# Seven products of quarters in place of eight for part of the second expert layer's first matrix

## The chip, the cores and the metric

The kernel runs on one core of a Trainium2 chip. The metric is the device time of one execution in microseconds (us), taken as the median over runs. TensorE multiplies matrices into PSUM; VectorE, ScalarE and GpSimd work on vectors; SyncE issues most DMAs. In the rows PE is TensorE's matmul, PEld its weight load, DVE is VectorE, ACT ScalarE, POOL GpSimd, SP SyncE.

## The reference

Windowed attention gives x with 2304 tokens of 512 features; two expert layers follow. The change lies in the second one:

```python
def _moe_ref(x, w_gate, w_val, w_out, rms_g):   # first layer, d_ff = 1536
    xn = x / sqrt(mean(x * x, -1) + 1e-06) * rms_g
    g = xn @ w_gate
    return (g * sigmoid(g) * (xn @ w_val)) @ w_out

def _moe2_ref(x, w_in, w_out, alpha):           # second layer, d_ff = 2048
    h = x @ w_in
    g = np.maximum(h, 0.0) + alpha * np.minimum(h, 0.0)
    return g @ w_out
```

## The kernel before

Every float32 matrix is held as a high and a low half in float16, and a product is three matmuls: high by high, high by low, low by high. Tokens go in blocks of up to 384 columns. Slot ("A", j, c) computes chunk c of the first layer for block j: 24 matmuls (`mm1`), then a chain over ACT, DVE (L921, L922), ACT (L924, high half) and POOL (L930, low half), then the output matmuls (`mm2`) two slots later. Weight blocks sit in slots of one SBUF buffer, `wb`.

The last stretch, the **end part**, does the second layer for the last 1024 tokens. It takes them as four pairs of 128-token tiles (t = 0 to 3) and the 2048 hidden features as eight pairs of 128-feature pieces (cp = 0 to 7), so 32 units in all. For each unit `mm3_t` multiplies by `w_in`: two pieces by 256 tokens, 12 matmuls of 256 columns for each piece. Where the two token tiles lie apart (t = 2), it is 24 matmuls of 128 columns for each piece. Then `mi` (L1080, ACT) and L1084, L1085 (DVE) apply the activation into a tile `fa`; L1086 to L1089 (DVE) form sums of quarters; L1092, L1094 (ACT) write high halves and L1093 (DVE), L1095 (POOL) low halves. `mm4_t` multiplies by `w_out` with seven products of quarters (Winograd's form of Strassen's scheme), 21 matmuls of 256 columns, three units later (`LAGT`). `out_t` (L1120 to L1127) joins the results of a token pair and writes them. `remake` prepares `w_out` for it once for each cp: two POOL adds (L1039, L1040), four DVE subtractions into `s` (L1042 to L1045), an ACT copy (L1048) and a DVE pass (L1049). These eight preparations run under the last "A" slots, one for each slot. `fa` has two buffers, `s` (tag `yb`) one, the PSUM pool `p3` four banks.

The order on each engine is made by a scheduler from the order of the code and its own estimates. The matmul calls of all stages have one line, L97.

## Time and profile before

| | us |
|---|---|
| median of 3 runs (954.62 to 957.86) | 954.78 |
| the profiled execution | 955.83 |
| its span | 953.9 |
| PE busy / DVE / ACT / POOL | 906.1 / 639.4 / 548.2 / 319.2 |

The span is the time from the first to the last instruction in the trace; 1.9 us of the profiled execution lie around it, and this execution is 1.05 us above the median. Rows below give starts in us from the beginning of the span.

### The profile page before, as it was taken

What the parts mean: (1) busy time and instruction counts of PE and PEld (TensorE: products, weight loads), DVE (VectorE), ACT (ScalarE), POOL (GpSimd) and SP (SyncE); (2) the same over time, 40 slices, a digit from 0 to 9 for tenths busy, and PEclk for the clock granted to TensorE, in tenths of its full rate; (3) what the DMA queues carried; (4) which work ended last, traced back from release to release, by engine and by line L of the source; (5) the groups of instructions that cost most, each with busy time, mean ns of one, the idle gap of its engine ahead of it and who ended that gap; (6) DMA issues with size and microseconds to landing.
All of it is one profiled execution on the core that took longest, in us unless ns stands there. A gap on an engine that the chain in (4) does not pass through costs nothing.

```text
span 953.9 us, 18814 instructions
## 1 busy us (share of the span) xinstructions
PE 906.1 (95%) x6760; PEld 618.7 (65%) x6760; DVE 639.4 (67%) x1569; ACT 548.2 (57%) x1537; POOL 319.2 (33%) x324
## 2 busy tenths in 40 slices
PE   6558799999999999999999999999999999999997
PEld 3447676775556676555555555555775558889986
DVE  5999897999777655554664765334545837777674
ACT  3426587766799967767665777544524324444342
POOL 2212441131354544332333233232253622322221
PEclk9687899999999999999999999999999999999999
DMA  9992446545436554544454653322301001000000
GB/s 255 324 360 81 120 132 188 142 157 140 81 72 108 98 103 77 123 83 95 110 90 74 114 106 72 67 59 42 55 14 23 1 1 35 1 23 24 2 24 23
DMA packets 191613, 88.14 MB, mean 92 GB/s; under 512 B 176800, under 2 KB 180384, under 8 KB 191520
## 3 DMA queue, kind: packets, MB, share of 16 engines
q1 hardware_dynamic: 189504, 83.27, 37.8%
q10 hardware_dynamic: 2016, 3.67, 1.1%
q8 instruction: 53, 0.87, 0.4%
q14 instruction: 40, 0.33, 0.1%
HBM read 55.32 MB, written 6.55 MB: 65 GB/s over the span
## 4 chain that ended last, share of the span: by engine, by line
PE 81%; DVE 9%; DMA 3%; issue 3%; ACT 1%; SPq 1%; POOL 1%; DVEq 0%; POOLq 0%; ACTq 0%
PE psw L97 40%; PE acc L97 24%; PE p L97 17%; DVE wb L232 2%; DVE wb L233 1%; DVE wb L231 1%; DVE wb L409 1%; SPq L629 1%; DMA wb<-in_q_dram 1%; PE psw L639 1%; DMA gs<-in_moe_rms_g_dram 1%; POOL ms L737 1%; ACT s L589 0%; DMA rkv<-in_v_dram 0%; DMA pT<-phl 0%
## 5 line engine op out<-in xcount | busy, mean ns | idle before, releaser
L97 PEld LDWEIGHTS <-wb 128*128 128x128 f16 (+1 forms) x4866 | 453.7, 99 | 196.3 <-DVE wb L233 18.6
L97 PE MATMUL psw<-xyall,wb 128*128 128x384 f16 (+1 forms) x2784 | 428.2, 304 | 2.0 <-DVE sqo L284 1.2
L97 PE MATMUL acc<-wb,hlall 128*128 128x512 f16 x822 | 197.6, 379 | 0.8 <-DVE yhl L965 0.6
L97 PEld LDWEIGHTS <-hlall 128*128 128x128 f16 x822 | 79.4, 98 | 80.7 <-POOL hlall L930 1.1
L930 POOL TENSOR_TENSOR hlall<-t,hlall 128x384 f16<-128x384 f32 (+1 forms) x58 | 58.4, 1007 | 148.5 <-ACT hlall L924 130.7
L97 PE MATMUL acc<-wb 128*128 128x512 f16 (+1 forms) x402 | 82.8, 351 | 16.2 <-DVE wb L233 16.1
L97 PE MATMUL p<-xyall,wb 128*128 128x256 f16 (+1 forms) x960 | 88.7, 251 | 0.0
L1095 POOL TENSOR_TENSOR wb<-fa,wb 128x640 f16<-128x640 f32 x32 | 45.5, 1422 | 111.4 <-ACT wb L1094 108.5
L97 PE MATMUL p<-wb 128*128 128x256 f16 x672 | 77.6, 273 | 0.0
L920 ACT ACTIVATE t<-psw,tsc 128x384 f32<-128x384 f32 (+1 forms) x84 | 44.1, 525 | 56.0 <-PE psw L97 54.9
L921 DVE SCALAR_TENSOR_TENSOR t<-t,psw 128x384 f32<-128x384 f32 (+1 forms) x84 | 41.1, 489 | 48.6 <-ACT t L920 48.6
L589 ACT ACTIVATE s<-s,mx 96x128 f32<-96x128 f32 (+2 forms) x132 | 50.1, 380 | 19.9 <-DVE mx L581 18.2
L404 ACT ACTIVATE wb<-wb,wsg 128x512 f16<-128x512 f32 x68 | 46.3, 710 | 16.8 <-DVE wsg L341 10.2
L1093 DVE SCALAR_TENSOR_TENSOR wb<-fa,wb 128x384 f16<-128x384 f32 x32 | 40.5, 1269 | 22.2 <-ACT wb L1092 22.1
L1094 ACT ACTIVATE wb<-fa 128x640 f16<-128x640 f32 x32 | 23.5, 735 | 55.0 <-DVE fa L1087 55.0
L705 POOL TENSOR_TENSOR phl<-s,phl 96x512 f16<-96x512 f32 (+2 forms) x33 | 35.8, 1084 | 57.6 <-ACT phl L699 40.8
L930 POOL TENSOR_TENSOR hlall<-p,hlall 128x256 f16<-128x256 f32 (+1 forms) x49 | 39.3, 805 | 45.1 <-ACT hlall L987 42.0
L985 DVE SCALAR_TENSOR_TENSOR p<-m,oma,psw 128x256 f32<-128x256 f32 (+1 forms) x64 | 34.7, 542 | 26.7 <-ACT m L984 25.3
L407 POOL TENSOR_TENSOR wb<-wb 128x512 f16<-128x512 f32 x28 | 37.3, 1337 | 42.8 <-ACT wb L406 17.2
L930 POOL TENSOR_TENSOR wb<-t,wb 128x256 f16<-128x256 f32 (+1 forms) x26 | 27.2, 1047 | 71.5 <-ACT wb L924 71.5
L233 DVE SCALAR_TENSOR_TENSOR wb<-wb 128x512 int32<-128x512 int32 (+1 forms) x56 | 49.7, 891 | 0.3
L924 ACT ACTIVATE hlall<-t 128x384 f16<-128x384 f32 (+1 forms) x58 | 27.7, 477 | 37.8 <-DVE t L922 37.8
(201 smaller groups left out, 1320.0 us busy)
## 6 DMA issues: line engine op xcount, KB each, us to landing
wb<-in_moe_w_out_dram SPq DMA_DIRECT2D x28, 512.0 KB, 4.7
wb<-in_moe_w_in_dram SPq DMA_DIRECT2D x16, 512.0 KB, 3.8
wb<-in_moe_w_gate_dram SPq DMA_DIRECT2D x12, 512.0 KB, 6.7
wb<-in_moe_w_val_dram SPq DMA_DIRECT2D x12, 512.0 KB, 6.8
...
```

The source lines that it names most:

```text
L97: nc.tensor.matmul(o, a, b, start=start, stop=stop)
L233: nc.vector.scalar_tensor_tensor(w, r[:, :, :, 0], 29, w, ALU.logical_shift_right, ALU.bitwise_or)
L404: nc.scalar.activation(half(b, 0), dec(b), ACTF.Copy, scale=wsg[:, s:s + 1])
L407: nc.gpsimd.tensor_tensor(half(b, 1), dec(b), half(b, 0), ALU.subtract)
L589: nc.scalar.activation(s[:nq, h, :nk], s[:nq, h, :nk], ACTF.Exp, bias=mx[:nq, 1, h:h + 1], scale=-1.0, accum_out=g["dn"][:nq, h])
L705: nc.gpsimd.tensor_tensor(phl[:nq, 1, :, :nk], g["s"][:nq, :, :nk], phl[:nq, 0, :, :nk], ALU.subtract)
L920: nc.scalar.activation(t[:, :T], pg[:, :T], ACTF.Tanh, scale=tsc[:, chunk(c):chunk(c) + 1])
L921: nc.vector.scalar_tensor_tensor(t[:, :T], t[:, :T], 1.0, pg[:, :T], ALU.add, ALU.mult)
L930: nc.gpsimd.tensor_tensor(a[:, 1, :T], t[:, :T], a[:, 0, :T], ALU.subtract)
L985: nc.vector.scalar_tensor_tensor(p[:, :T], m[:, :T], oma[:, c:c + 1], ps[:, :T], ALU.mult, ALU.add)
L1093: nc.vector.scalar_tensor_tensor(l[:, 0:3], f[:, 0:3], 0.25, h[:, 0:3], ALU.mult, ALU.subtract)
L1095: nc.gpsimd.tensor_tensor(l[:, 3:8], f[:, 3:8], h[:, 3:8], ALU.subtract)
```

## The change

For cp = 2, 3, 4 (`SEVEN`) `mm3_t` no longer does eight products of quarters but seven (`seven`): 42 matmuls of 128 columns into two PSUM banks, `pa` and `pb`. ACT copies one product out (L1119) and DVE adds the others up (L1120 to L1123) into the `fa` tile; the activation then reads that SBUF tile. The scheme needs combinations of the weights, once for each of the three cp (`remake_in`), and of the tokens, once for each t (`remake_y`: the low half of these is made on POOL). For t = 0 these are made together with the eight old preparations, now twelve in all, and three of the last "A" slots may take two; for t = 1 to 3 the tokens are prepared at cp = 5 of the pair before. One of the five buffers for the halves of a unit moves to `hlall`, and f[:, 7] is computed from other, equal terms.

```diff
@@ -1050,6 +1050,79 @@
         ts[cp] = [x.rearrange("p (a c) -> p a c", a=4) for x in (h, l)]
 
 
+    SEVEN = range(2, 5)
+    ws, yt4, slot_of = {}, {}, {}
+
+    def split4(s, eng=nc.vector):
+        at_ = one_slot(), one_slot()
+        h, l = (wb16[:, i * 1024:(i + 1) * 1024] for i in at_)
+        sv = s.rearrange("p a c -> p (a c)")
+        nc.scalar.activation(h, sv, ACTF.Copy)
+        eng.tensor_tensor(l, sv, h, ALU.subtract)
+        r = [x.rearrange("p (a k c) -> p a k c", a=4, c=128) for x in (h, l)]
+        for x, i in zip(r, at_):
+            slot_of[id(x)] = i
+        return r
+
+    def remake_in(cp):
+
+        c, c_ = b_i(2 * cp), b_i(2 * cp + 1)
+        f = tail["tl"].tile([128, 4, 256], F32, tag="fa", bufs=2, name="f")
+        s = tail["tl"].tile([128, 7, 256], F32, tag="yb", bufs=1, name="s")[:, 0:4]
+        fv = f.rearrange("p a c -> p (a c)")
+        nc.gpsimd.tensor_tensor(fv[:, 0:512], half(c, 0), half(c, 1), ALU.add)
+        nc.gpsimd.tensor_tensor(fv[:, 512:1024], half(c_, 0), half(c_, 1), ALU.add)
+        a11, a12, a21, a22 = (f[:, i] for i in range(4))
+        nc.vector.tensor_tensor(s[:, 0], a21, a22, ALU.add)
+        nc.vector.tensor_tensor(s[:, 1], s[:, 0], a11, ALU.subtract)
+        nc.vector.tensor_tensor(s[:, 2], a11, a21, ALU.subtract)
+        nc.vector.tensor_tensor(s[:, 3], a12, s[:, 1], ALU.subtract)
+        ws[cp] = split4(s)
+
+    def y_parts(t):
+        (j0, n0), (j1, n1) = tiles[2 * t:2 * t + 2]
+        return [xy[j % NXY][:, :, :, n * 128:n * 128 + 128] for j, n in ((j0, n0), (j1, n1))]
+
+    def remake_y(t):
+
+        f = tail["tl"].tile([128, 2, KD, 128], F32, tag="fa", bufs=2, name="f")
+        s = tail["tl"].tile([128, 7, 256], F32, tag="yb", bufs=1, name="s")[:, 0:4]
+        for i, y in enumerate(y_parts(t)):
+            nc.gpsimd.tensor_tensor(f[:, i], y[:, 0], y[:, 1], ALU.add)
+        b11, b12, b21, b22 = (f[:, i, 2 * k:2 * k + 2].rearrange("p a c -> p (a c)") for k in range(2) for i in range(2))
+        nc.vector.tensor_tensor(s[:, 0], b12, b11, ALU.subtract)
+        nc.vector.tensor_tensor(s[:, 1], b22, s[:, 0], ALU.subtract)
+        nc.vector.tensor_tensor(s[:, 2], b22, b12, ALU.subtract)
+        nc.vector.tensor_tensor(s[:, 3], b21, s[:, 1], ALU.subtract)
+        yt4[t] = split4(s, nc.gpsimd)
+
+    def seven(t, cp):
+        pa = tail["ps3"].tile([128, 4, 128], F32, tag="p3", name="pa")
+        pb = tail["ps3"].tile([128, 4, 128], F32, tag="p3", name="pb")
+        y0, y1 = y_parts(t)
+        c, c_ = b_i(2 * cp), b_i(2 * cp + 1)
+        w, y = ws[cp], yt4[t]
+        for o, wl, yl in (
+                (pa[:, 0], lambda l, k: blk(c, l)[:, k], lambda l, k: y0[:, l, k]),
+                (pa[:, 1], lambda l, k: blk(c, l)[:, 2 + k], lambda l, k: y0[:, l, 2 + k]),
+                (pa[:, 2], lambda l, k: w[l][:, 1, k], lambda l, k: y[l][:, 1, k]),
+                (pb[:, 1], lambda l, k: w[l][:, 0, k], lambda l, k: y[l][:, 0, k]),
+                (pb[:, 2], lambda l, k: w[l][:, 2, k], lambda l, k: y[l][:, 2, k]),
+                (pb[:, 0], lambda l, k: blk(c_, l)[:, 2 + k], lambda l, k: y[l][:, 3, k]),
+                (pb[:, 3], lambda l, k: w[l][:, 3, k], lambda l, k: y1[:, l, 2 + k])):
+            n = 0
+            for k in range(2):
+                for l, m in ((0, 0), (0, 1), (1, 0)):
+                    mm(o, wl(l, k), yl(m, k), n == 0, n == 5)
+                    n += 1
+        f = tail["tl"].tile([128, 8, 128], F32, tag="fa", bufs=2, name="fa")
+        nc.scalar.activation(f[:, 0], pa[:, 0], ACTF.Copy)
+        nc.vector.tensor_tensor(f[:, 1:6:4], pa[:, 1:3], f[:, 0:1].to_broadcast([128, 2, 128]), ALU.add)
+        nc.vector.tensor_tensor(f[:, 6:8], pb[:, 1:3], f[:, 5:6].to_broadcast([128, 2, 128]), ALU.add)
+        nc.vector.tensor_tensor(f[:, 2:4], pb[:, 0:2], f[:, 7:8].to_broadcast([128, 2, 128]), ALU.add)
+        nc.vector.tensor_tensor(f[:, 4], pb[:, 3], f[:, 6], ALU.add)
+        return f
+
...
@@ -1060,33 +1133,42 @@
 
     def mm3_t(t, cp):
         tl = tail["tl"]
-        ps = tail["ps3"].tile([128, 2, 256], F32, tag="p3", name="p3")
...
+        if cp in SEVEN:
+            f = seven(t, cp)
+            psv = f[:, 1:5]
+            one, two = psv[:, 0:4:3], psv[:, 1:3]
         else:
-            parts = [(128 * i, 128, xy[j % NXY][:, :, :, n * 128:n * 128 + 128]) for i, (j, n) in enumerate(((j0, n0), (j1, n1)))]
-        for i in range(2):
-            b = b_i(2 * cp + i)
-            for col, w, yt in parts:
-                n = 0
-                for kc in range(KD):
-                    for l, m in ((0, 0), (0, 1), (1, 0)):
-                        mm(ps[:, i, col:col + w], blk(b, l)[:, kc, :], yt[:, m, kc, :], n == 0, n == 3 * KD - 1)
-                        n += 1
...
+            f = None
...
+            psv = ps.rearrange("p a (n c) -> p (a n) c", n=2)
+            one, two = psv[:, 0:2], psv[:, 2:4]
 
         mi = tl.tile([128, 4, 128], F32, tag="mi", bufs=2, name="mi")
-        psv = ps.rearrange("p a (n c) -> p (a n) c", n=2)
         nc.scalar.activation(mi, psv, ACTF.Relu, scale=-1.0)
 
-        f = tl.tile([128, 8, 128], F32, tag="fa", bufs=2, name="fa")
+        m1, m2 = (mi[:, 0:2], mi[:, 2:4]) if f is None else (mi[:, 0:4:3], mi[:, 1:3])
+        if f is None:
+            f = tl.tile([128, 8, 128], F32, tag="fa", bufs=2, name="fa")
         c = 2 * cp
-        nc.vector.scalar_tensor_tensor(f[:, 1:5:3], mi[:, 0:2], oma[:, c:c + 1], psv[:, 0:2], ALU.mult, ALU.add)
-        nc.vector.scalar_tensor_tensor(f[:, 2:4], mi[:, 2:4], oma[:, c + 1:c + 2], psv[:, 2:4], ALU.mult, ALU.add)
+        nc.vector.scalar_tensor_tensor(f[:, 1:5:3], m1, oma[:, c:c + 1], one, ALU.mult, ALU.add)
+        nc.vector.scalar_tensor_tensor(f[:, 2:4], m2, oma[:, c + 1:c + 2], two, ALU.mult, ALU.add)
         nc.vector.tensor_tensor(f[:, 5], f[:, 4], f[:, 3], ALU.add)
         nc.vector.tensor_tensor(f[:, 6], f[:, 5], f[:, 1], ALU.subtract)
         nc.vector.tensor_tensor(f[:, 0], f[:, 2], f[:, 6], ALU.subtract)
-        nc.vector.tensor_tensor(f[:, 7], f[:, 1], f[:, 4], ALU.subtract)
+        nc.vector.tensor_tensor(f[:, 7], f[:, 3], f[:, 6], ALU.subtract)
         a = tail["a"].popleft()
         h, l = (x.rearrange("p (a c) -> p a c", a=8) for x in a)
         nc.scalar.activation(h[:, 0:3], f[:, 0:3], ACTF.Copy, scale=0.25)
@@ -1261,7 +1343,15 @@
         pump_to(N0 * (n + 1) // first)
     for b in w1[:2]:
         split_w(b)
-    units = deque(range(NP))
+    LAGT = 3
+    units = deque(sorted([(cp + LAGT, 1, cp) for cp in range(NP)] + [(cp, 0, cp) for cp in SEVEN] + [(SEVEN[0], 2, 0)]))
+
+    def make_unit():
+        _, which, n = units.popleft()
+        (remake_in, remake, remake_y)[which](n)
+
+    TWO = (4, 7, 10)
+
     for s in slots:
         kind, j, c = s
         for f in take(dur(s) * (PACE if (kind, j) == ("A", 2) else 1.0)):
@@ -1295,27 +1385,35 @@
         last = c == (C1 if kind == "A" else C2) - 1
         early_one = kind == "A" and j in ahead and c < LOOK
         flush(kind, j, 0 if last else LAG0 if (kind, j) == ("A", 0) else LOOK if early_one else LAG)
-        if (kind, j) == ("A", NJ - 1) and c and units and sum(free) >= 2:
-            remake(units.popleft())
+        if (kind, j) == ("A", NJ - 1):
+            for _ in range(1 + (c in TWO)):
+                if units and sum(free) >= 2:
+                    make_unit()
 
     ps_stack.close()
     tail["ps4"] = ctx.enter_context(tc.tile_pool(name="ps4", bufs=1, space=PSUM))
     tail["ps3"] = ctx.enter_context(tc.tile_pool(name="ps3", bufs=4, space=PSUM))
     give(*given)
     nc.vector.tensor_scalar(rct, rct, k1, 4.0, ALU.mult, ALU.mult)
+    NY = 5
     order = [(t, cp) for t in range(NT) for cp in range(NP)]
-    LAGT = 3
     behind = deque()
     for n in range(len(order) + 1):
         if n < len(order):
             t, cp = order[n]
-            while units and units[0] <= cp:
-                remake(units.popleft())
             if n == 0:
-                tail["a"] = deque((slot16(), slot16()) for _ in range(LAGT + 2))
+                flat = hlall.rearrange("p n a t -> p (n a t)")
+                tail["a"] = deque([(flat[:, 0:1024], flat[:, 1024:2048])] + [(slot16(), slot16()) for _ in range(LAGT + 1)])
+            if cp == NY and t < NT - 1:
+                remake_y(t + 1)
+            while units and units[0][0] <= cp:
+                make_unit()
             mm3_t(t, cp)
             if units:
-                remake(units.popleft())
+                make_unit()
+            if cp == NP - 1:
+                for x in yt4.pop(t):
+                    give(slot_of.pop(id(x)))
             behind.append((t, cp))
         while behind and (n == len(order) or len(behind) > LAGT + (behind[0][1] == 0 < behind[0][0])):
             t, cp = behind.popleft()
```

Three places in the order. **VectorE, where the last "A" slots end.** `t_...` are the slots' products (one pair L921, L922 for each slot), `s_...` the combinations. Before:

```order
L1049 SCALAR_TENSOR_TENSOR wb_72<-s_9220,wb_72 128x1024
L921 SCALAR_TENSOR_TENSOR t_9153<-t_9153,psw_9127 128x384
L922 SCALAR_TENSOR_TENSOR t_9153<-t_9153,psw_9128 128x384
L921 SCALAR_TENSOR_TENSOR t_9204<-t_9204,psw_9178 128x384
L922 SCALAR_TENSOR_TENSOR t_9204<-t_9204,psw_9179 128x384
L921 SCALAR_TENSOR_TENSOR t_9255<-t_9255,psw_9229 128x384
L922 SCALAR_TENSOR_TENSOR t_9255<-t_9255,psw_9230 128x384
L921 SCALAR_TENSOR_TENSOR t_9296<-t_9296,psw_9270 128x384
L922 SCALAR_TENSOR_TENSOR t_9296<-t_9296,psw_9271 128x384
```

After:

```order
L1049 SCALAR_TENSOR_TENSOR wb_72<-s_9291,wb_72 128x1024
L921 SCALAR_TENSOR_TENSOR t_9275<-t_9275,psw_9249 128x384
L1042 TENSOR_TENSOR s_9301<-f_9300 128x256
L1044 TENSOR_TENSOR s_9301<-f_9300 128x256
L922 SCALAR_TENSOR_TENSOR t_9275<-t_9275,psw_9250 128x384
L1043 TENSOR_TENSOR s_9301<-f_9300,s_9301 128x256
L1045 TENSOR_TENSOR s_9301<-f_9300,s_9301 128x256
L1049 SCALAR_TENSOR_TENSOR wb_72<-s_9301,wb_72 128x1024
L921 SCALAR_TENSOR_TENSOR t_9336<-t_9336,psw_9310 128x384
L922 SCALAR_TENSOR_TENSOR t_9336<-t_9336,psw_9311 128x384
```

The last four pairs L921, L922 stood alone; now preparations stand between them, the last one directly ahead of the last pair.

**VectorE, where the first units of the end part meet the last first-layer output.** L965 reads the last of the accumulators, whose banks `mm4_t` needs. `fa_9398` and `fa_9438` are the first unit, `fa_9436` and `fa_9476` the second. Before:

```order
L1305 TENSOR_SCALAR rct_104<-rct_104,k1_100 128x8
L1084 SCALAR_TENSOR_TENSOR fa_9436<-mi_9434,oma_76,p3_9409 128x2x128
L1085 SCALAR_TENSOR_TENSOR fa_9436<-mi_9434,oma_76,p3_9409 128x256
L1093 SCALAR_TENSOR_TENSOR wb_72<-fa_9398,wb_72 128x384
L1089 TENSOR_TENSOR fa_9436<-fa_9436 128x128
L1086 TENSOR_TENSOR fa_9436<-fa_9436 128x128
L965 SCALAR_TENSOR_TENSOR yhl_9352<-acc_8858,sg_9330,yhl_9352 128x512
L1084 SCALAR_TENSOR_TENSOR fa_9474<-mi_9472,oma_76,p3_9447 128x2x128
```

After:

```order
L1175 SCALAR_TENSOR_TENSOR hlall_103<-fa_9438,hlall_103 128x384
L1168 TENSOR_TENSOR fa_9476<-fa_9476 128x128
L1397 TENSOR_SCALAR rct_104<-rct_104,k1_100 128x8
L1169 TENSOR_TENSOR fa_9476<-fa_9476 128x128
L965 SCALAR_TENSOR_TENSOR yhl_9392<-acc_8858,sg_9370,yhl_9392 128x512
L1170 TENSOR_TENSOR fa_9476<-fa_9476 128x128
L1171 TENSOR_TENSOR fa_9476<-fa_9476 128x128
L1120 TENSOR_TENSOR fa_9531<-pa_9487,fa_9531 128x2x128
L1121 TENSOR_TENSOR fa_9531<-pb_9488,fa_9531 128x256
```

L965 keeps its place among the second unit's sums; behind it now come the additions of the first unit with seven products. On PE, `mm4_t` of the first unit now stands behind the fourth `mm3_t`; before it stood in the middle of the fifth.

**ScalarE in the later units.** L1094 and L1092 became L1176 and L1174. Before:

```order
L1080 ACTIVATE mi_11295<-p3_11270 128x512
L1094 ACTIVATE wb_72<-fa_11297 128x640
L1092 ACTIVATE wb_72<-fa_11297 128x384
L1080 ACTIVATE mi_11354<-p3_11329 128x512
L1094 ACTIVATE wb_72<-fa_11356 128x640
L1092 ACTIVATE wb_72<-fa_11356 128x384
```

After:

```order
L1174 ACTIVATE wb_72<-fa_11430 128x384
L1176 ACTIVATE wb_72<-fa_11430 128x640
L1160 ACTIVATE mi_11498<-fa_11492 128x512
L1174 ACTIVATE wb_72<-fa_11492 128x384
L1176 ACTIVATE wb_72<-fa_11492 128x640
L1160 ACTIVATE mi_11581<-p3_11556 128x512
L1174 ACTIVATE wb_72<-fa_11583 128x384
L1176 ACTIVATE wb_72<-fa_11583 128x640
```

The three columns that DVE waits for (L1092, now L1174) are written first; in the units with seven products `mi` reads the `fa` tile.

## Rows read from the trace of the kernel before

**Rows 1.** The page: PE's busy time, and TensorE's granted clock in 40 slices.

```profile
PE 906.1 (95%) x6760; PEld 618.7 (65%) x6760; DVE 639.4 (67%) x1569; ACT 548.2 (57%) x1537; POOL 319.2 (33%) x324
...
PEclk9687899999999999999999999999999999999999
```

**Rows 2.** Stretches: length, then busy us of PE, PEld, DVE, ACT, POOL; clock; DMA.

```profile
750.00:760.00 10.00, 10.00 (x60) 5.68 (x58) 8.47 (x14) 3.27 (x6) 6.72 (x5) 1.00 0.00 0
...
770.00:782.30 12.30, 12.30 (x72) 6.81 (x71) 2.22 (x4) 2.79 (x5) 1.82 (x2) 1.00 0.01 1
...
861.00:900.00 39.00, 39.00 (x547) 37.18 (x546) 27.18 (x59) 15.25 (x27) 11.29 (x8) 1.00 0.05 16
...
938.00:954.00 16.00, 9.05 (x83) 7.87 (x81) 5.94 (x13) 3.55 (x6) 1.40 (x1) 0.85 0.14 34
```

**Rows 3.** Timeline of PE in the end part: start, duration, operation, count.

```profile
816.72 2.78 PE L97 MATMUL p<-xyall,wb 128*128 128x256 f16 x24
...
819.34 2.46 PE L97 MATMUL p<-wb 128*128 128x256 f16 x21
...
860.93 2.84 PE L97 MATMUL p<-xyall,wb 128*128 128x128 f16 x48
...
863.61 2.46 PE L97 MATMUL p<-wb 128*128 128x256 f16 x21
...
865.90 2.84 PE L97 MATMUL p<-xyall,wb 128*128 128x128 f16 x48
```

**Rows 4.** Timeline of DVE under the last "A" slots.

```profile
744.76 1.26 DVE L1049 SCALAR_TENSOR_TENSOR wb<-s,wb 128x1024 f16<-128x1024 f32 x1 [0.66 <-ACT wb L1048]
...
755.58 1.84 DVE L1049 SCALAR_TENSOR_TENSOR wb<-s,wb 128x1024 f16<-128x1024 f32 x1 [1.12 <-ACT wb L1048]
...
761.44 1.22 DVE L1049 SCALAR_TENSOR_TENSOR wb<-s,wb 128x1024 f16<-128x1024 f32 x1 [1.12 <-ACT wb L1048]
...
765.91 1.23 DVE L1049 SCALAR_TENSOR_TENSOR wb<-s,wb 128x1024 f16<-128x1024 f32 x1 [0.66 <-ACT wb L1048]
...
782.30 0.55 DVE L921 SCALAR_TENSOR_TENSOR t<-t,psw 128x384 f32<-128x384 f32 x1 [4.01 <-ACT t L920]
```

**Rows 5.** Timeline of POOL at the same place.

```profile
755.19 1.15 POOL L1039 TENSOR_TENSOR f<-wb 128x512 f32<-128x512 f16 x1
756.30 2.14 POOL L1040 TENSOR_TENSOR f<-wb 128x512 f32<-128x512 f16 x1
```

**Rows 6.** Timeline of ACT, POOL, PE and DVE where the end part begins.

```profile
784.17 0.52 ACT L924 ACTIVATE wb<-t 128x384 f16<-128x384 f32 x1 [1.90 <-DVE t L922]
...
784.84 0.91 POOL L930 TENSOR_TENSOR wb<-t,wb 128x384 f16<-128x384 f32 x1 [5.00 <-ACT wb L924]
...
788.03 2.11 PE L97 MATMUL acc<-wb 128*128 128x512 f16 x9
...
799.97 0.74 DVE L965 SCALAR_TENSOR_TENSOR yhl<-acc,sg,yhl 128x512 f16<-128x512 f32 x1
...
801.00 2.46 PE L97 MATMUL p<-wb 128*128 128x256 f16 x21
```

**Rows 7.** Timeline of POOL and DVE in the end part.

```profile
816.03 1.40 POOL L1095 TENSOR_TENSOR wb<-fa,wb 128x640 f16<-128x640 f32 x1 [2.83 <-ACT wb L1094]
...
816.40 1.44 DVE L1093 SCALAR_TENSOR_TENSOR wb<-fa,wb 128x384 f16<-128x384 f32 x1 [0.95 <-ACT wb L1092]
...
817.77 0.47 DVE L1084 SCALAR_TENSOR_TENSOR fa<-mi,oma,p 128x256 f32<-128x256 f32 x1
...
820.63 1.45 DVE L1093 SCALAR_TENSOR_TENSOR wb<-fa,wb 128x384 f16<-128x384 f32 x1 [0.95 <-ACT wb L1092]
```

**Rows 8.** Timeline of DVE and PE where two token pairs meet.

```profile
838.49 0.42 DVE L1127 TENSOR_TENSOR yo<-p,yo 128x256 f32<-128x256 f32 x1
...
841.61 4.75 PE L97 MATMUL p<-wb 128*128 128x256 f16 x42
```

**Rows 9.** Weight loads of the end part by form: count, busy us, mean ns.

```profile
L97 PEld LDWEIGHTS <-wb 128*128 128x128 f16 x1523 | 132.9, 98 | 12.9
```

17 lines of the change are left out of this document (14 added, 3 removed).

## The prediction

> **What bounds the kernel now.** I read the page first: PE is busy 906 of 954 us, and its granted clock is at the upper level, 2.4 GHz, in all slices but the first few [rows 1]. Then a table of stretches, to see whether that holds where the change lies: from 750 us on PE is busy without a gap at clock 1.00, and only the last 16 us, where the output drains, are not full [rows 2]. So until about 947 us every matmul removed is time gained, and every wait that PE meets is time lost. The other engines matter only by making PE wait. DVE is nearest to that: 8.5 of 10 us under the last "A" slots and 27.2 of 39 in the end part [rows 2], part of it blocked time, as shown below. From 770 us to the end of the first layer it is nearly idle, 2.2 of 12.3 us [rows 2]; that is where the new preparations go.
>
> **TensorE's work.** A unit's first product takes 24 matmuls of 256 columns from 816.72 to 819.34, 2.62 us. Where the token tiles lie apart, 48 of 128 columns take 2.68 us, from 860.93 to 863.61, each with its own weight load [rows 3]. That is 55.8 ns for a matmul of 128 columns in just the form that the change uses, weights loaded beside it. So 42 take 2.34 us. In t = 0, 1 and 3 a unit saves 0.28 us, nine units 2.5; in t = 2 it saves six matmuls, 0.335 us, three units 1.0. **In all 3.5 us**, and there is no more to gain, since the rest of PE's work and the drain stay as they are. The counted saving of an eighth of the columns is met by the half-length matmuls almost exactly, because these cost 55.8 ns and not more than half of 109.
>
> The Trainium skill (TensorE: Matmul & The Clock Gate, section Back-to-back issue gap) gives 81 ns for a sustained pair of weight load and 128-column matmul. By it 42 would take 3.40 us and the change would lose some 7 us in t = 0, 1, 3 and win 1.5 in t = 2. The trace does not agree, with its 55.8 ns over 48 in a row [rows 3].
>
> **Preparations.** Before there are eight; now there are twelve: three combinations of weights (the same kinds of operations as the old ones) and one of tokens, whose low half goes to POOL. The order keeps the first four at their places; the fourth ends at about 746.0 (744.76 and 1.26 [rows 4]). Eight follow, before four. They must be through by 782.30, when DVE wants to begin the last slot's product [rows 4]: 36.3 us. From one L1049 to the next it took 5.86 us (755.58 to 761.44) where POOL added for the next one, and 4.47 (761.44 to 765.91) where it had nothing left to add; each holds one pair L921, L922 [rows 4]. The difference is blocking: L1049 at 755.58 took 1.84 us instead of 1.22, until just after POOL's first add ended, and POOL's second add, started at 756.30, took 2.14 instead of 1.15 [rows 4, 5]. Eight at 4.47, less one pair of 0.9 that they do not hold, are 34.9 us: no delay. Eight at 5.86 are 46.0: 9.7 us late. I take six at 5.5, near the upper row since POOL's adds run under nearly all of them, and the last two at 4.47: 41.0, and so 4.7 us late. PE has some slack there: the last slot's high half was ready at 784.69 and its matmuls began at 788.03 [rows 6], 3.3 us later. **Cost 1.4 us, between 0 and 6.4.** Queued behind the late DVE are L921, L922, then ACT's and POOL's halves, and PE waits for these.
>
> **Start of the end part.** The first `mm4_t` began at 801.00, just after L965 ended at 800.71 [rows 6]; L965 frees accumulator banks. PE now gets there earlier: without 12 matmuls of 256 columns (1.31 us) and with two shorter units (0.55), so at 799.15. L965 stands as late as before in DVE's queue. Where the first bank is one that L965 frees, PE waits 1.55 us; where another frees it, nothing. I take the middle, **0.8 us**.
>
> **The units themselves.** Each unit with seven products adds on DVE the passes L1120 to L1123 over 896 PSUM columns; at 0.42 us for 256 [rows 8] that is 1.5 us, and one more wait for ACT (`mi` now comes after them), for which the 0.95 us before L1093 [rows 7] is the upper bound and 0 the lower. The tokens' combination adds four passes, 1.7 us, and on POOL two adds (1.15 each [rows 5]) and a pass over 1024 columns; scaled from 1.40 for 640 [rows 7] I estimate 2.2. Against that stands what DVE has to spare: when behind, it did a unit in 4.23 us (L1093 to L1093, 816.40 to 820.63 [rows 7]), while PE's takes 2.62 + 2.29 = 4.91 [rows 3]. Also, the wait of 0.95 before L1093 should shrink, as ACT now writes those three columns first. `mm4_t` comes three units later, so a backlog of several us hides. The order of PE where two token pairs meet puts two units with seven products (4.7 us) ahead of the next `mm4_t`; before, its banks were free at about 838.9 and wanted at 841.61 [rows 8], 2.7 us of slack, and PE comes 0.55 us sooner. I take **0.4 us** for all of that, between 0 and the price in the third rival. The drain behind the last matmul is that of before.
>
> **Sum.** -3.5 + 1.4 + 0.8 + 0.4 = -0.9 us. Set against the profiled execution, 955.83, that is 954.9; that execution is 1.05 above the median of the runs, so the median forecast is **953.9 us**.
>
> **Rivals.**
> *All covered.* DVE and POOL finish the eight preparations in time, and L965 is not what the first `mm4_t` waits for: 954.8 - 3.5 = 951.3. For it: DVE's 10 idle us of 12.3 ahead of 782 [rows 2]. Against: the pace of 5.86.
> *Full stalls at both junctions.* The preparations come 6.5 us late and cost 3.2, L965 costs 1.55, the end part 1: 957.1. For it: blocking runs in both directions [rows 4, 5].
> *VectorE becomes the bound of the end part, and the kernel is slower.* If the loop of 4.23 us stays as it is, a token pair takes 8 x 4.23 + 2.7 (`out_t`) + 3 x 2.45 + 1.7 = 45.6 us of DVE, against PE's 8 x 4.91 - 0.85 = 38.4. That is 7 us late in each of three pairs and 5.5 in the last, 27 in all, less some 8 that the lag of three units takes up once (3 x 4.91, less a unit's own chain, put at 6 to 7): 19, and 970. The point from which it decides is a mean of some 4.8 us of DVE for a unit, PE's own. ACT's new order should give back some 0.6 us a unit, 5 a pair, which leaves 2 a pair and hardly a stall; half of that relief gives about 962, the price I use. For it also: L1093 takes 1.44 us when POOL's op runs beside it [rows 7], and the activation of the new units reads two SBUF tiles, where L1084 read PSUM and took 0.47 right after [rows 7].
> The Trainium skill (SBUF — State Buffer, section Who interferes with whom) says that a VectorE instruction with two SBUF inputs and a GpSimd one that reads SBUF block each other fully. The trace agrees for L1093, which ends 0.4 us after POOL's op; by that rule the six activations of a token pair may each wait up to 1.4 us, by the row of L1084 none, and no run yet shows this form of them.
> *Weight loads set the pace.* A load's row lasts 98 ns in the mean [rows 9]; if 42 of them could not overlap, a unit would take 4.12 us, and twelve would lose 18: 972. The 48 in 2.68 us [rows 3] speak against it.
>
> **How the numbers follow.** What a measurement of this kernel can tell from no change is about 0.5%, 4.8 us: 950.0 to 959.6. Forecast 0.45, all covered 0.25, full stalls 0.15, VectorE the bound 0.13, weight loads 0.02. The first three lie within 0.5%; of VectorE the bound I leave a fifth to milder cases within it, so slower has 0.12, same 0.87, and faster 0.01, since PE has only 3.5 us to give. The range, from just below all covered to just above full stalls, 950.9 to 958.0, holds 0.85.
>
> **What would show it.** A unit of seven should show 42 matmuls in 2.34 us. A gap of PE ahead of the last first-layer output matmuls, and one ahead of the first `mm4_t`, would show the two junction costs; PE idle ahead of `mm4_t` of units three to five, released by POOL or DVE, the third rival. Wrong would be the sum if 128-column matmuls ran slower with `wb` as the moving operand, or if DVE's blocking at POOL were of another size than in these rows.

## The result, and the profile after

The changed kernel took 962.31 us (median; 961.11 to 962.46), the kernel before, timed again on the same chip, 956.32 (954.62 to 958.40). The ratio is 1.0063, with an interval of 1.0048 to 1.0079: slower by about 6 us, where no change was forecast. The profiled execution has a span of 960.5 us against 953.9. All ratios here leave out executions that ran at a lower granted clock from end to end, such as the profiled one of e14 (0.66).

The page of the changed kernel, busy time and instructions for each engine, to be read against [rows 1]:

```profile
PE 907.0 (94%) x6904; PEld 618.1 (64%) x6904; DVE 667.8 (70%) x1648; ACT 557.0 (58%) x1556; POOL 347.4 (36%) x342
```

PE is busy 0.9 us longer, although its units of seven are shorter; part of that is matmuls at a lower clock, which count as busy for longer. DVE has 28 us more, POOL 28, ACT 9. The stretches, in the columns of [rows 2]:

```profile
801.00:840.00 39.00, 36.76 (x397) 33.07 (x395) 33.59 (x82) 17.27 (x33) 17.73 (x12) 1.00 0.06 11
...
880.00:920.00 40.00, 39.13 (x490) 36.24 (x488) 33.03 (x78) 16.56 (x31) 15.86 (x12) 1.00 0.04 15
```

In the end part DVE went from 27.18 of 39 us [rows 2] to about 33 of 40, and PE, which had no gap, now has 2.2 us of gaps in one stretch and 0.9 in another. What PE waited for between 700 and 970 us (total us, times, longest); in the trace of before this view has no line:

```profile
PE acc L97 <- ACT hlall L924: 2.0, 1, 2.0
PE p L97 <- DVE yhl L965: 1.5, 1, 1.5
PE p L97 <- DVE yo L1208: 1.1, 2, 0.5
PE p L97 <- POOL hlall L1177: 0.7, 1, 0.7
PE p L97 <- DVE yo L1209: 0.7, 2, 0.4
PE acc L97 <- POOL hlall L930: 0.4, 1, 0.4
PE p L97 <- DVE t L922: 0.2, 1, 0.2
```

Three places, then: the last first-layer output matmuls (L924, L930, and L922 for the first second-layer matmuls, which stand among them), the first `mm4_t` (L965), and the end part (L1208, L1209, L1177).

**How the stages are counted.** The part of the program ahead of the change varies by some us from one execution to the next, so all kernels are compared by PE's timeline from one mark: the start of the last first-layer block's matmuls (a group of 55, at 721.86 in before and 721.55 in after). *A* runs from there to the start of the last output matmuls of the first layer (788.03 in before [rows 6]), *B* on to the start of the first `mm4_t` (801.00 [rows 6]), *C* on to PE's end.

| kernel | A | B | C | sum | against before | ratio of times (95%) |
|---|---|---|---|---|---|---|
| before | 66.17 | 12.97 | 145.88 | 225.02 | | 1 |
| after | 71.13 | 12.76 | 148.11 | 232.00 | +6.98 | 1.0063 (1.0048 to 1.0079) |
| e1 preparations only | 70.84 | 13.00 | 146.21 | 230.05 | +5.03 | 1.0046 (1.0030 to 1.0062) |
| e2 no preparations | 66.17 | 12.67 | 144.26 | 223.10 | -1.92 | 0.9973 (0.9958 to 0.9989) |
| e3 no additions | 70.44 | 12.85 | 143.76 | 227.05 | +2.03 | 1.0017 (0.9996 to 1.0038) |
| e9 no later tokens' preparation | 70.45 | 12.69 | 144.26 | 227.40 | +2.38 | 1.0039 (1.0021 to 1.0057) |
| e5 preparations early | 72.31 | 12.68 | 148.14 | 233.13 | +8.11 | 1.0075 (1.0048 to 1.0101) |
| e8 weight adds on DVE | 67.06 | 12.89 | 148.19 | 228.14 | +3.12 | 1.0051 (1.0038 to 1.0063) |
| e6 two units, 3 and 4 | 68.23 | 12.69 | 145.23 | 226.15 | +1.13 | 1.0015 (1.0003 to 1.0026) |
| e7 two units, 3 and 5 | 68.23 | 12.69 | 144.95 | 225.87 | +0.85 | 1.0024 (1.0010 to 1.0039) |
| e10 as e7, weight adds on DVE | 66.17 | 12.68 | 144.94 | 223.79 | -1.23 | 0.9990 (0.9979 to 1.0001) |
| e11 all preparation on DVE | 66.35 | 12.69 | 144.77 | 223.81 | -1.21 | 0.9978 (0.9967 to 0.9988) |
| e12 tokens' preparation on POOL | 67.05 | 13.01 | 150.02 | 230.08 | +5.06 | 1.0060 (1.0041 to 1.0079) |
| e13 units 3, 5, 7, weight adds on DVE | 67.69 | 14.06 | 141.21 | 222.96 | -2.06 | 0.9975 (0.9961 to 0.9989) |
| e15 units 3, 5, 7 | 72.37 | 15.27 | 141.20 | 228.84 | +3.82 | 1.0027 (1.0012 to 1.0042) |
| e16 units 3, 5, 7, all on DVE | 66.36 | 12.77 | 144.33 | 223.46 | -1.56 | 0.9971 (0.9960 to 0.9981) |

The sums of single executions and the ratios agree to within 2 us. So a difference of 1 us between two sums is not more than a hint, while the waits that PE shows in a stage are read to 0.1 us.

**The gain is there in full.** One unit of seven products in PE's timeline of the changed kernel, and the start of the next unit (start, duration, count):

```profile
842.69 0.83 PE L97 MATMUL pa<-xyall,wb 128*128 128x128 f16 x12
...
845.04 0.83 PE L97 MATMUL pa<-xyall,wb 128*128 128x128 f16 x12
```

42 matmuls from 842.69 to 845.04 are 2.35 us (forecast 2.34), also with `wb` as the moving operand. What three places take back is 10.5 us. A is 5.0 longer. Ahead of the first `mm4_t`, PE's unit is through at 803.81 (six matmuls of 55.8 ns from 803.47 on) and the next row starts 1.6 later:

```profile
803.47 0.50 PE L97 MATMUL pb<-xyall,wb 128*128 128x128 f16 x6
805.44 2.45 PE L97 MATMUL p<-wb,hlall 128*128 128x256 f16 x21 [1.47 <-DVE yhl L965]
```

C is 3.85 longer than in e2, where PE meets no wait in it. With -3.5 the sum is +6.95, against +6.98 in the table.

### The profile page after: what moved, and what is told of

The parts are those of the page before. It is cut to its first block, busy times and chain, and to the rows that moved or that the text cites. A ratio compares the mean times of both kernels' runs of the same rounds, so it can differ in the third digit from the quotient of the medians.

```text
span 960.5 us, 19207 instructions
## 1 busy us (share of the span) xinstructions
PE 907.0 (94%) x6904; PEld 618.1 (64%) x6904; DVE 667.8 (70%) x1648; ACT 557.0 (58%) x1556; POOL 347.4 (36%) x342
## 4 chain that ended last, share of the span: by engine, by line
PE 65%; DVE 19%; issue 5%; DMA 5%; ACT 4%; POOL 2%; SPq 1%; DVEq 0%; ACTq 0%; POOLq 0%
PE psw L97 34%; PE acc L97 22%; PE p L97 7%; DVE wb L232 2%; DVE wb L233 2%; DMA wb<-in_moe_w_out_dram 1%; DVE wb L231 1%; DVE wb L409 1%; DVE wb L1049 1%; DVE t L922 1%; ACT wb L1048 1%; DVE t L921 1%; SPq L629 1%; DVE fa L1166 1%; DVE fa L1167 1%
## 5 line engine op out<-in xcount | busy, mean ns | idle before, releaser
L97 PEld LDWEIGHTS <-wb 128*128 128x128 f16 (+1 forms) x4863 | 438.9, 99 | 197.5 <-DVE wb L233 18.5
L97 PEld LDWEIGHTS <-hlall 128*128 128x128 f16 x969 | 93.4, 98 | 87.8 <-ACT hlall L924 2.5
L930 POOL TENSOR_TENSOR hlall<-t,hlall 128x384 f16<-128x384 f32 (+1 forms) x58 | 58.1, 1003 | 140.1 <-ACT hlall L924 122.2
L921 DVE SCALAR_TENSOR_TENSOR t<-t,psw 128x384 f32<-128x384 f32 (+1 forms) x84 | 41.0, 488 | 41.2 <-ACT t L920 41.2
L97 PE MATMUL p<-wb 128*128 128x256 f16 x525 | 61.6, 273 | 1.8 <-DVE yo L1208 1.1
L1177 POOL TENSOR_TENSOR wb<-fa,wb 128x640 f16<-128x640 f32 x25 | 35.9, 1436 | 66.0 <-ACT wb L1176 49.6
L97 PE MATMUL p<-xyall,wb 128*128 128x256 f16 (+1 forms) x600 | 56.7, 253 | 0.2 <-DVE t L922 0.2
L930 POOL TENSOR_TENSOR hlall<-p,hlall 128x256 f16<-128x256 f32 (+1 forms) x49 | 39.2, 803 | 44.0 <-ACT hlall L987 40.8
L930 POOL TENSOR_TENSOR wb<-t,wb 128x256 f16<-128x256 f32 (+1 forms) x26 | 27.2, 1047 | 69.5 <-ACT wb L924 69.5
L737 POOL TENSOR_TENSOR ms<-ms,mhalf 96x1 f32<-96x1 f32 (+2 forms) x24 | 17.2, 718 | 95.8 <-DVE ms L736 84.1
L924 ACT ACTIVATE hlall<-t 128x384 f16<-128x384 f32 (+1 forms) x58 | 27.7, 477 | 39.8 <-DVE t L922 39.8
L233 DVE SCALAR_TENSOR_TENSOR wb<-wb 128x512 int32<-128x512 int32 (+1 forms) x56 | 49.2, 881 | 0.3
L232 DVE SCALAR_TENSOR_TENSOR wb<-wb 128x512 int32<-128x512 int32 (+1 forms) x56 | 47.4, 851 | 0.2
```

What stands on the lines that cost most here:

```text
L97: nc.tensor.matmul(o, a, b, start=start, stop=stop)
L232: nc.vector.scalar_tensor_tensor(w, r[:, :, :, 1], -0x40000000, w, ALU.bitwise_and, ALU.bitwise_or)
L233: nc.vector.scalar_tensor_tensor(w, r[:, :, :, 0], 29, w, ALU.logical_shift_right, ALU.bitwise_or)
L921: nc.vector.scalar_tensor_tensor(t[:, :T], t[:, :T], 1.0, pg[:, :T], ALU.add, ALU.mult)
L930: nc.gpsimd.tensor_tensor(a[:, 1, :T], t[:, :T], a[:, 0, :T], ALU.subtract)
L1177: nc.gpsimd.tensor_tensor(l[:, 3:8], f[:, 3:8], h[:, 3:8], ALU.subtract)
```

## The experiments

**e1: the preparations alone.** All units keep the old product; the combinations are made and not used.

```diff
-        if cp in SEVEN:
+        if cp in ():
```

> All preparations of the changed kernel, but all units with eight products as before (the prepared combinations are not used). Theory (three separate losses: about 4.5 us because the preparations end late, 1.6 us at the first mm4 behind L965, 3.7 us of PE gaps in the end part because DVE has the additions): the last first-layer output matmuls of PE begin 4 to 5 us later than in the kernel before (788.0), the end part has no gaps of more than 1 us, span 958 to 959.5. Rival (the units with seven products cost the time, the preparations are hidden): span 954 to 955, last output matmuls at 788.

A is 4.7 us longer than before, B and C hardly differ (+0.03, +0.33). The preparations alone cost nearly all of A's loss, and hardly anything in the end part. The span, 962.8 us, lies above the expected one because the part ahead of the mark took 4 us longer in this execution.

**e2: the units without the preparations.** The seven products read the given blocks and tokens in place of their combinations; everything that makes combinations is left out.

```diff
-        w, y = ws[cp], yt4[t]
+        w = [wb16[:, hl_at[b] * 1024:(hl_at[b] + 1) * 1024].rearrange("p (a k c) -> p a k c", a=4, c=128) for b in (c, c_)]
...
-    units = deque(sorted([(cp + LAGT, 1, cp) for cp in range(NP)] + [(cp, 0, cp) for cp in SEVEN] + [(SEVEN[0], 2, 0)]))
+    units = deque((cp + LAGT, 1, cp) for cp in range(NP))
```

> Units with seven products, but the combinations of weights and tokens are not made: existing blocks stand in for them. The eight old preparations stay. Theory: last output matmuls at 788 as before, the wait behind L965 stays (0.5 to 1.6 us), gaps of 2 to 3 us in the end part stay since the additions stay; span 953.5 to 955.5. Rival (the units cost it): span near that of the changed kernel, 959 to 961. If DVE's additions cost nothing alone: 951 to 952.

Measured -1.92 us, ratio 0.9973. A is that of before, and of PE's waits one line is left:

```profile
PE p L97 <- DVE yhl L965: 1.4, 1, 1.4
```

So -3.5 and 1.57 for L965 (from 801.92, where the unit ahead ends, to 803.49). The gaps of 2 to 3 us that were expected to stay in the end part are not there. The additions of the units, by themselves, cost nothing: those gaps need the preparations too.

**e3: no additions.** The units leave L1119 to L1123 out, and the activation reads the bank `pb`.

```diff
-        nc.scalar.activation(f[:, 0], pa[:, 0], ACTF.Copy)
-        nc.vector.tensor_tensor(f[:, 1:6:4], pa[:, 1:3], f[:, 0:1].to_broadcast([128, 2, 128]), ALU.add)
...
-        nc.vector.tensor_tensor(f[:, 4], pb[:, 3], f[:, 6], ALU.add)
-        return f
+        return pb
```

> Changed kernel without ACT's copy and DVE's four additions in the units with seven products: the activation reads one PSUM bank of products directly. Theory (DVE's additions cause the gaps of the end part): the 4.5 us at the end of the first layer stay, the gaps at the first mm4_t after out_t and at 830 us go; span 955.5 to 957.5. Rival (the tokens' preparation and POOL's blocking cause the gaps): gaps stay, span 959.5 to 960.5.

The loss of A stays, but for 0.7 us (70.44; see the last section), that of C is gone (143.76). The edit takes away one thing more than additions: the activation now reads PSUM, where in the changed kernel its first pass L1166 reads two SBUF tiles and took 1.26 us beside POOL's L1177 (at 850.62). **e9** leaves out the other half: the tokens' preparation for t = 1 to 3, whose units then use that of t = 0.

```diff
-            if cp == NY and t < NT - 1:
-                remake_y(t + 1)
...
-                for x in yt4.pop(t):
-                    give(slot_of.pop(id(x)))
+                yt4[t + 1] = yt4.pop(t)
```

> Changed kernel without the preparations of the tokens for t = 1 to 3: the combination of t = 0 is used throughout. Theory (the tokens' preparation on top of the additions fills DVE and POOL): the wait of 4.6 us at the end of the first layer and that behind L965 stay, the gaps of the end part (about 3.7 us) fall under 1 us; span 956.5 to 957.5 where the changed kernel's is 960.5. Rival (the additions alone are enough): gaps stay at 2 us or more.

C is 144.26: gone as well. Additions and tokens' preparation must both be there for the end part's gaps. Which property of theirs makes the gaps was open; see e11 to e15.

**e5: preparations earlier.** In the last block the weight blocks that are done with are given back earlier, so that the preparations can begin and double up earlier.

```diff
-            for b in (b_g(c), b_v(c), b_o(c)):
-                give(hl_at.pop(b))
+            give(hl_at.pop(b_o(c)))
...
-    TWO = (4, 7, 10)
+    TWO = (3, 5, 7)
...
+            if j == NJ - 1:
+                give(hl_at.pop(b_g(c)), hl_at.pop(b_v(c)))
```

> Changed kernel, but the gate and value blocks of the last first-layer block are given free right after their last matmuls instead of after the output matmuls, so that the preparations can begin about two slots sooner; the slots that may take two are 3, 5, 7. Theory (the twelve preparations are too late because each takes about 5.5 us from a start set by free slots): the last L921 of the first layer comes at or before 786 instead of 789.95, PE's wait there falls from 4.5 us to under 1, span 955.5 to 957. Rival (something else at that place, such as the order of the last pairs, sets the wait): span as the changed kernel, 960 to 961.

This failed: A grew to 72.31. The preparations were through 2.2 us sooner (the last DVE pass began 65.05 us after the mark, in the changed kernel 67.26), but the wait ahead of the last output matmuls became 3.1 us: the L922 of the slot before the last stood behind that pass, and its high half (L924) ended 1.4 us later than in the changed kernel. So the order among preparations and the slots' own passes counts too, and beginning sooner is no cure by itself.

**e8: GpSimd's adds on VectorE.** The two adds of each weight preparation move; VectorE has more to do.

```diff
-        nc.gpsimd.tensor_tensor(fv[:, 0:512], half(c, 0), half(c, 1), ALU.add)
-        nc.gpsimd.tensor_tensor(fv[:, 512:1024], half(c_, 0), half(c_, 1), ALU.add)
+        nc.vector.tensor_tensor(fv[:, 0:512], half(c, 0), half(c, 1), ALU.add)
+        nc.vector.tensor_tensor(fv[:, 512:1024], half(c_, 0), half(c_, 1), ALU.add)
```

> Changed kernel with the two adds of each weight preparation on DVE in place of POOL. Theory (DVE and POOL block each other for whole operations, so a preparation's pace is the sum of POOL's 2.3 us, DVE's 2.5 us and the slot's own 0.9): without POOL's adds DVE fills its wait for ACT with them, the pace falls from 5.5 to 4.6 to 5.0 us, the last L921 comes at 782 to 786 and PE's wait there falls under 1 us; time 4 to 5 us below the changed kernel. Rival (DVE's own time is what is short): the pace grows to 6 us or more and the wait to 8 us.

A fell from 71.13 to 67.06: L922 of the last slot came 3.4 us sooner, and the clock did not fall there, which is the other 0.7 (last section). The timelines show why L922 came sooner. The changed kernel, POOL and then DVE over one preparation:

```profile
772.30 1.16 POOL L1039 TENSOR_TENSOR f<-wb 128x512 f32<-128x512 f16 x1 [1.56 <-DVE s L1045]
773.41 2.14 POOL L1040 TENSOR_TENSOR f<-wb 128x512 f32<-128x512 f16 x1
```

```profile
773.28 1.26 DVE L1049 SCALAR_TENSOR_TENSOR wb<-s,wb 128x1024 f16<-128x1024 f32 x1 [0.66 <-ACT wb L1048]
774.64 1.19 DVE L1042 TENSOR_TENSOR s<-f 128x256 f32<-128x256 f32 x1
775.75 1.13 DVE L1044 TENSOR_TENSOR s<-f 128x256 f32<-128x256 f32 x1
776.80 0.41 DVE L1043 TENSOR_TENSOR s<-f,s 128x256 f32<-128x256 f32 x1
...
778.80 1.26 DVE L1049 SCALAR_TENSOR_TENSOR wb<-s,wb 128x1024 f16<-128x1024 f32 x1 [1.12 <-ACT wb L1048]
```

L1042 and L1044 take 1.19 and 1.13 us where L1043 takes 0.41 for as many columns, and POOL's L1040 takes 2.14 where L1039 takes 1.16: the two engines hold each other up (L1044 beside POOL's L930, a slot's low half, from 775.51 to 776.60). From L1049 to L1049 it is 5.52 us. In e8, DVE's adds and the subtractions behind them:

```profile
771.01 0.69 DVE L1039 TENSOR_TENSOR f<-wb 128x512 f32<-128x512 f16 x1
771.62 1.41 DVE L1040 TENSOR_TENSOR f<-wb 128x512 f32<-128x512 f16 x1
772.95 1.21 DVE L1049 SCALAR_TENSOR_TENSOR wb<-s,wb 128x1024 f16<-128x1024 f32 x1
774.19 0.42 DVE L1042 TENSOR_TENSOR s<-f 128x256 f32<-128x256 f32 x1
774.54 0.42 DVE L1044 TENSOR_TENSOR s<-f 128x256 f32<-128x256 f32 x1
...
777.80 1.22 DVE L1049 SCALAR_TENSOR_TENSOR wb<-s,wb 128x1024 f16<-128x1024 f32 x1
```

An add costs DVE 0.69 us when nothing holds it up, and L1042 and L1044 are back at 0.42: 4.85 us from L1049 to L1049, with a pair L921, L922 in it, which the 5.52 us above do not hold. Not every preparation gains as much: the eight last together took 40.80 us in e8 (L1049 at 746.39 to 787.19) and 43.96 in the changed kernel (744.85 to 788.81), with six pairs in both. C stays at 148.19, with the same waits on L1177, L1208 and L1209, so the adds of the weight preparations are not C's cause. The median says less than the stages: it lies 4.8 us above that of before, where the changed kernel's lay 6.0 above, and the two intervals overlap; 4 to 5 us less were expected.

**e6, e7: two units for a token pair**, side by side or apart, with GpSimd's adds.

```diff
-    SEVEN = range(2, 5)
+    SEVEN = (3, 4)
```

> Units with seven products for cp = 3, 4 only, otherwise the changed kernel: eleven preparations in place of twelve, eight units in place of twelve. Theory (twelve preparations at about 5.5 us each overrun by 7.7 us, of which PE forgives 3.3; DVE's end part is overfull only with three such units and the tokens' preparation together): the overrun is 2 us or so and PE does not wait for the last output matmuls, no gaps in the end part of more than 0.5 us, saved 2.3 us; span of the stage from the last output matmuls on 2 us shorter than before; time 0.1 to 0.3% below the kernel before. Rival (any preparation at this place costs PE in proportion): the wait falls from 4.6 to 3 us only, time equal to or above the kernel before.

e7 has `SEVEN = (3, 5)` there.

> As the kernel with two, but cp = 3 and 5, so that no two such units stand next to each other. Theory (DVE's total load decides, not neighbourhood): equal to the kernel with cp = 3, 4 within 1 us. Rival (neighbouring units are what backs DVE up): up to 1 us better.

With one preparation less A is 68.23 in both, still 2.06 more than before: the preparations are late even then, where no wait was expected. C has no gaps in either. **e10** is e7 with the adds on VectorE as in e8:

> Two units (cp = 3 and 5) of a token pair with seven products, and the POOL adds of all preparations on VectorE. Counted from the first matmuls of the last first-layer block. If the preparations are paced by VectorE and GpSimd blocking each other, eleven of them without GpSimd's adds are through nearly in time: the gap of TensorE ahead of the last first-layer output matmuls is 0 to 0.4 us (it was 2.06 with the same two units and GpSimd's adds), and the end part is as there, 144.95. The sum is 223.9 to 224.2 against 225.02 of the kernel before: about 1 us faster than before. If the gap comes from the number of VectorE's own passes, it stays near 2 and the time is 0.5 to 1 us above before.

A is exactly that of before, 66.17, and the sum -1.23 (the interval of the times just reaches 1). That the pace of the preparations makes A's loss is shown twice now, with three units (e8) and with two.

**e11, e12: where the tokens' preparation runs.** Both are e8, and move all of `remake_y` onto one engine, in e11 VectorE.

```diff
-            nc.gpsimd.tensor_tensor(f[:, i], y[:, 0], y[:, 1], ALU.add)
+            nc.vector.tensor_tensor(f[:, i], y[:, 0], y[:, 1], ALU.add)
...
-        yt4[t] = split4(s, nc.gpsimd)
+        yt4[t] = split4(s)
```

> Three units with seven products, the adds of all weight preparations on VectorE as in e8, and now the tokens' preparation wholly on VectorE too: its two adds and its low half leave GpSimd. Three theories of the 3.7 us that TensorE waits in the end part. Load: VectorE has too much to do between cp = 5 and the junction of two token pairs; then 2.5 us more of VectorE's work a pair make the gaps longer, and the end part takes 149 to 152 us (148.2 in e8). Blocking: GpSimd's adds and low half beside VectorE's passes cost the time; then the gaps shrink, 144.5 to 146. Place: the two units with seven products that stand in a row ahead of the junction's output matmuls take away TensorE's slack; then they stay about as they are, 148.

In e12 the four subtractions go to GpSimd.

```diff
-        nc.vector.tensor_tensor(s[:, 0], b12, b11, ALU.subtract)
+        nc.gpsimd.tensor_tensor(s[:, 0], b12, b11, ALU.subtract)
...
-        nc.vector.tensor_tensor(s[:, 3], b21, s[:, 1], ALU.subtract)
+        nc.gpsimd.tensor_tensor(s[:, 3], b21, s[:, 1], ALU.subtract)
```

> As e8, but the tokens' preparation wholly on GpSimd: its four subtractions leave VectorE. Load: VectorE is rid of 1.7 us a pair, as where the preparation was left out, and the gaps go: end part 144 to 145.5 us. Blocking: GpSimd works longer beside VectorE's passes, and the gaps stay or grow: 148 to 150. Place: about 148.

More work on VectorE made C 3.4 us shorter than in e8 (144.77); less work on VectorE made it 1.8 longer (150.02). VectorE's load is thus not the cause by itself; GpSimd's work beside VectorE's is one. At the meeting of the second and third token pair in the changed kernel, PE and DVE (L1208 frees the bank that PE waits for):

```profile
885.98 1.15 PE L97 MATMUL p<-wb 128*128 128x256 f16 x9
887.63 0.50 PE L97 MATMUL p<-wb 128*128 128x256 f16 x3 [0.51 <-DVE yo L1208]
888.49 3.44 PE L97 MATMUL p<-wb 128*128 128x256 f16 x30 [0.36 <-DVE yo L1209]
```

```profile
849.58 0.55 DVE L1175 SCALAR_TENSOR_TENSOR hlall<-fa,hlall 128x384 f16<-128x384 f32 x1
...
865.04 2.10 DVE L1170 TENSOR_TENSOR fa<-fa 128x128 f32<-128x128 f32 x1
...
874.90 0.56 DVE L1175 SCALAR_TENSOR_TENSOR hlall<-fa,hlall 128x384 f16<-128x384 f32 x1 [0.39 <-ACT hlall L1174]
...
887.16 0.41 DVE L1208 TENSOR_TENSOR yo<-p,yo 128x256 f32<-128x256 f32 x1
```

The same in e11:

```profile
883.82 4.75 PE L97 MATMUL p<-wb 128*128 128x256 f16 x42
```

```profile
847.13 0.55 DVE L1175 SCALAR_TENSOR_TENSOR hlall<-fa,hlall 128x384 f16<-128x384 f32 x1
...
859.26 1.64 DVE L1061 TENSOR_TENSOR wb<-s,wb 128x1024 f16<-128x1024 f32 x1
...
869.48 0.56 DVE L1175 SCALAR_TENSOR_TENSOR hlall<-fa,hlall 128x384 f16<-128x384 f32 x1 [0.39 <-ACT hlall L1174]
...
881.75 0.41 DVE L1208 TENSOR_TENSOR yo<-p,yo 128x256 f32<-128x256 f32 x1
```

Every fifth unit writes its halves to `hlall`. Between two such writes, with one tokens' preparation among the five units, the changed kernel took 25.32 us and e11 22.35. In the former a sum of quarters, L1170, stood 2.10 us for 0.29 of work while POOL's low half L1061 ran (864.73 to 866.98). L1167 and L1168 took 1.37 and 1.12 us for 0.47 and 0.29 while POOL's adds L1091 ran (856.45 to 858.96). How much of the 3.0 us between the two kernels each of these makes was not measured. L1208 began 1.2 us behind PE's start of the output matmuls, in e11 2.1 ahead.

**e13, e15: where the three units stand.** cp = 3, 5, 7, in e13 with e8's adds on VectorE, in e15 in the changed kernel as it is.

```diff
-    SEVEN = range(2, 5)
+    SEVEN = (3, 5, 7)
```

> Three units with seven products, cp = 3, 5 and 7 in place of 2, 3, 4, with the adds of the weight preparations on VectorE as in e8. The additions of three units and the tokens' preparation are all there, but at the junction of two token pairs TensorE no longer has two units with seven products in a row ahead of the output matmuls that want the banks. Place: the gaps go, end part 143.7 to 145, and the whole is 223.5 to 224.7 against 225.02 of before, 0.3 to 1.5 us faster than before. Load: VectorE has as much to do as in e8, the end part takes 147 to 148.5 and the whole is 2 to 3 us slower than before.

> The changed kernel with only the place of the three units altered: cp = 3, 5, 7 in place of 2, 3, 4; GpSimd keeps all its adds. Place as a cause by itself: the waits on the output tiles at the junctions of token pairs and the wait for L965 go; the first mm4_t to the end takes 141 to 142.5 with some 1.1 us more ahead of it, and the gap ahead of the last first-layer output matmuls stays at 4.5 to 6, since GpSimd paces the preparations as before: 226.5 to 228.5 in all against 232.00, slower than before by 1.5 to 3.5 us. If GpSimd's additions beside the preparations were the cause of the end part's gaps too, the gaps stay and the whole is 229 to 232.

Additions and tokens' preparation are all there, GpSimd's share too, and C has no gap in either. A is 72.37 in e15, 1.2 longer than the changed kernel's, as L922 came 1.2 later still. B is 1.2 longer than in e13: nine of its matmuls ran at the lower clock, in 3.20 us and not 2.11, and with that the sum lies just above the expected 228.5. PE's waits in e15 are all at the last output matmuls:

```profile
PE acc L97 <- ACT hlall L924: 2.3, 1, 2.3
PE p L97 <- DVE t L922: 1.1, 1, 1.1
PE acc L97 <- POOL hlall L930: 0.6, 1, 0.6
```

The wait for L965 is gone too, since the first `mm4_t` now stands one unit further back. B and C of e13 are 155.27 together, of before 158.85: 3.58 less, the whole gain of TensorE. At the junction of e15, PE and DVE:

```profile
887.50 4.75 PE L97 MATMUL p<-wb 128*128 128x256 f16 x42
```

```profile
885.88 0.42 DVE L1208 TENSOR_TENSOR yo<-p,yo 128x256 f32<-128x256 f32 x1
```

L1208 ends 1.2 us ahead of PE's arrival, without any change in what GpSimd does. Place and GpSimd's work are thus two conditions of one gap: taking away either is enough, as taking away the additions or the tokens' preparation was.

**e16: all at once**, units 3, 5, 7 and all preparations on VectorE. Its first run (e14) gave the time 954.93 us, ratio 0.9977 (0.9965 to 0.9989); the stages are those of a second run.

> Units cp = 3, 5, 7 with seven products and all preparations, weights and tokens, on VectorE alone. If the change's loss is the sum of its causes as found (preparations paced by GpSimd, the order at the junctions, GpSimd's work for the tokens), nothing of it is left here: a gap of 0 to 0.5 us ahead of the last first-layer output matmuls, no gap in the end part, and TensorE's whole gain of 3.5 us stays: 221.4 to 222.3 against 225.02 of before, ratio 0.996 to 0.998. If a cause is still missing, more than 1 us of the gain is not there: 222.6 or above.

> The kernel of e14 once more, since that run's profile caught an execution at a clock of 0.66 from end to end and its stages cannot be compared. Expected as for e14: 221.4 to 222.3 in the stages against 225.02 if the causes found are the whole loss, 222.6 or above if one is missing.

A is 66.36, but the sum is 223.46, not 221.4 to 222.3. That missed: two waits are left.

```profile
PE p L97 <- DVE yhl L965: 0.8, 1, 0.8
PE p L97 <- POOL hlall L1177: 0.6, 1, 0.6
```

In its order the first `mm4_t` stands 23 matmuls sooner than in e13, and meets L965 again. Counted by PE's timeline the two cost 0.94 and 0.78 us, and A 0.19: 1.9 us, which with -3.5 makes the -1.56 seen. No loss is left without a wait that explains it, but the causes are not independent: mending one moves the order, and the order brings another back. The time is 954.34 us against 956.46, ratio 0.9971: 0.3% **faster than the kernel before**, and so faster than the changed one, as are e11 and e13.

## Why the prediction failed, point by point

- **TensorE, -3.5 us: right.** 2.35 us for a unit, and 3.58 less in the stages of e13 where nothing waits. The weight-load rival and the price of 81 ns are out.
- **Preparations, +1.4: mis-sized, 5.0.** The pace is the step that failed. I put 41.0 us for eight preparations; they took 43.9 (from the end of L1049 at 744.85 to the end of the one at 788.81). I let the last two go at 4.47 us each, since POOL had nothing to add for them; from L1049 to L1049 they took 5.27 and 4.74, and POOL's L1040 still ran under the first of them (778.93 to 781.08). I had also misread the row of L1049 at 755.58: it ended at 757.42, not just after POOL's first add (756.34) but 1.1 us later, so it had waited for the whole add. The slack, 3.3 us, was about right, but at another pass: what PE met last was not the high half but L922, for which the first matmuls of `mm3_t` wait. Before, then after:

```profile
783.58 0.56 DVE L922 SCALAR_TENSOR_TENSOR t<-t,psw 128x384 f32<-128x384 f32 x1 [0.72 <-PE psw L97]
...
787.27 0.93 PE L97 MATMUL p<-xyall,wb 128*128 128x256 f16 x7
```

```profile
790.60 0.56 DVE L922 SCALAR_TENSOR_TENSOR t<-t,psw 128x384 f32<-128x384 f32 x1
```

Before, L922 ended 3.1 us ahead of these matmuls. From the common mark it ended 7.3 us later in the changed kernel, and 7.3 - 3.1 = 4.2. The other 0.7 of A is a fall of the clock (last section), for which the sum had no term.
- **L965, +0.8: at its upper end, 1.6.** I took the middle between two ends where no row spoke for a middle: the bank is one that L965 frees or it is not. the waits for L965 in e2 (1.4), e11 (1.4) and the changed kernel (1.5) show that it is.
- **The end part, +0.4: mis-sized, 3.85.** It is 1.1 us at L1177 in the first token pair, 1.2 and 1.5 at the second and third junction. The relief that I expected from ACT's new order came: units behind time followed each other in 3.63 us (L1175 at 871.27 and 874.90), not 4.23, and units of seven in 4.74 (889.75 and 894.49). What failed is that I weighed the tokens' preparation by its passes, 1.7 us, and not by what POOL's part of it does to the passes beside it. Five units with one such preparation took 25.32 us, 5.06 each, above the 4.8 that I had put as the deciding point. The place was the one I had named, two units of seven ahead of the next `mm4_t`; that it would use up 2.7 us of slack I did not carry through.
- **The rivals.** The time, 962.3, lies at the third rival's lower price, but that was not its mechanism alone: PE lost 5.0 us ahead of the end part and 3.85 in it. "Full stalls at both junctions" named the right places, with L965 at its size (1.55) but the preparations at 3.2 for 5.0 and the end part at 1 for 3.85. The third rival left open whether the activations of the new units are held up. They are, in part: L1166 took 1.26 and 1.25 us beside POOL's L1177 (at 850.62 and 855.40); reading PSUM it took 0.47 beside the same (e11, 858.48). The row of L1084 that I set against it could not show this, since it began at 817.77, after POOL's pass had ended at 817.43 [rows 7].
- **The range.** Its upper end followed the rival of full stalls and not the upper ends of the terms. Two terms went high together, 5.0 and 3.85, and both have GpSimd's work beside VectorE's passes as a cause, the first in the weights' preparation, the second in the tokens'.

The Trainium skill (SBUF — State Buffer, section Who interferes with whom) says that the two engines lock one pair of ports against each other. The trace agrees, with 1.19 for 0.41 us on DVE and 2.14 for 1.16 on POOL. I had used that rule for the third rival; for the first term I had only the pace of one interval, and let two preparations go without any blocking.
